# A four-layer attention kernel: Wo read in three rows a partition straight from its input, another set of streamed weight halves, local weights loaded in the second step, one local layer in the last two steps

## The chip, the cores and the metric

The kernel runs on one core of one Trainium2 chip. The metric is the device time of one execution in microseconds. A core has a matrix engine (PE, with its weight loads shown apart as PEld), DVE (VectorE), ACT (ScalarE), POOL (GpSimd), and SP (SyncE), which here only issues DMAs; sixteen DMA engines move data between the DRAM of the chip (HBM) and the on-chip memory (SBUF). PE writes its results to PSUM.

## The reference

The input x has 2048 rows of 640. Four layers follow each other, each with a layernorm ahead and the sum with its input behind:

```
def _A_ref(x, mem0, Wq, Wk, Wv, Wo, seg_len):      # H=32 heads, Dh=192, M=8, seg_len=32
    mem = mem0
    for s in range(n_seg):                          # 64 segments, one after the other
        h = concatenate([mem, xs], axis=1)          # 8 memory rows + 32 rows of x
        q, k, v = h @ Wq, h @ Wk, h @ Wv
        p = softmax(where(mask, q k^T * scale, -1e9))
        o = einsum('bhte,hed->btd', p v, Wo)
        mem = o[:, :M]; outs.append(o[:, M:])
def _B_ref(x, wqkv, wo):                            # 32 heads of 20, each row sees 8 rows,
    ...                                             # itself and every second one before it
x = x + _A_ref(_layernorm(x), ...); x = x + _B_ref(_layernorm(x), ...)
x = x + _A_ref(_layernorm(x), ...); x = x + _B_ref(_layernorm(x), ...)
```

Both A layers use the same weights, and both B layers too. A segment of an A layer needs the memory rows that the segment before it has made, so that the 64 segments are a chain.

## The kernel before

All data stand transposed, with the 640 features on 5 x 128 partitions. One step handles two segments at once: segment s of the first pair of layers (l = 0) and segment s - 2 of the second pair (l = 1, `LAG` = 2); every A matmul has 2 x 40 columns. There are 67 steps: 0 to 65 do the A layers ("attend"), 1 to 66 do the B layers for what the step before has left ("local"). Step 66 has local work alone.

The A weights are 4 x 7.5 MB and do not fit in SBUF beside the rest. They are cut into 64 halves of 128 x 1920 values (480 KB): 0 to 31 are Wk and Wq by turns, 32 to 47 Wv, 48 to 63 Wo. Of these 31 stay in SBUF from step 0 on (`res`), and 33 are streamed in every step through a ring of five buffers (`ring`, tile `wt`, `RING` = 5). Which ones are streamed is worked out by `resident_halves` (L88), which spreads them evenly over the columns that PE has to work through. In step 0, `half` (L242) loads every half from the input with `load_direct` (L238), and POOL writes each streamed one to a DRAM tile `Wr` (L253), from which the later steps read it in one run a partition (L255). A load for Wq, Wk or Wv from the input has rows of 768 bytes, one for Wo rows of 1,280 bytes.

The order of PE and SP is written out by hand: `ORDER` (L53) lists the stages of a step, and PE and SP issue in the order of that list. `q` is one pair of halves of Wk and Wq (L333, evicted by ACT at L335), `s` the scores of four of them with the softmax (L355 to L363 on DVE, exponent on ACT L359), `t` the transposition of the probabilities (PE L370, copied by DVE L372 and ACT L373 to `PT`), `v` one half of Wv (L381; the copy to `vt` is on ACT, L385, for even ones and on DVE, L387, for odd ones), `pv` probabilities times v (L398, evicted by ACT L401 to `ot`), `o` the output projection (L415), which adds up over the whole step in PSUM. `finish_step` (L418) copies the new memory rows to `ST` (L426) and makes `xr` (L439) at the end. The local stages are `ln1` (L443), `qkv` (L449; the product of q with the eight shifted k, `prod`, is on DVE for l = 0 and on POOL for l = 1, L470), `logits` (L473), `e0` to `e4` (L502: PE L505, DVE L508 and L510) and `wo` (L512). `ln2` makes the second A layer's input (L317), and `store` writes out four segments (L537). Every fourth step the next 128 rows of x are loaded to `x_sb` (L266, issued by SP at the step's beginning) and normalized in the step after (`input_tile`, L268: statistics on DVE, L274 and L275, root on ACT, L260 and L261). On DVE, ACT and POOL the order is the scheduler's: it may put an operation ahead of others that stand before it in the program.

SP issues in order: a load of a streamed half waits until PE has done with the half that was loaded five streamed halves before, and whatever stands behind it waits too. The local weights `wqkv` and `wo` are loaded at the very beginning (L571, L572), ahead of all A weights.

Of the kernel before, what the change touches and what calls it, by code (L numbers as in the profile page):

```python
# [10 lines left out]
BF16 = mybir.dt.bfloat16  # L11
# [9 lines left out]
P = 128  # L21
D = 640
# [51 lines left out]
COLUMNS = {"q": 1200, "v": 1920, "o": 1200, "s": 2000, "pv": 1000, "t": 700, "ln1": 900, "ln2": 900, "qkv": 5000, "logits": 1000, "e": 500, "wo": 1700}  # L74


def halves_of(what, i):

    if what == "q":
        return [2 * i, 2 * i + 1]  # L80
    if what == "v":
        return [32 + i]
    if what == "o":
        return [48 + i] if i < 14 else [62, 63]
    return [None]


def resident_halves():  # L88

    order, t = [], 0  # L90
    for what, i in PLAN:
        for h in halves_of(what, i):
            t += COLUMNS.get(what, 0)
            if h is not None:
                order.append((h, t))
    kept, n = set(), 0
    for h, at in order:
        if (N_HALVES - N_RESIDENT) * at >= (n + 0.5) * t:
            n += 1
        else:  # L100
            kept.add(h)
    assert len(kept) == N_RESIDENT
    return kept


RESIDENT = resident_halves()
# [9 lines left out]
def window1(ap, c):  # L116

    v = ap[:, c, :, 0:SEG]
    dims = [list(x) for x in v.ap]
    return bass.AP(v.tensor, v.offset, dims[:2] + [[BDIL, BW]] + dims[2:])  # L120
# [12 lines left out]
class Kernel:  # L133
# [94 lines left out]
    def source(self, h):  # L228
        if h < 32:
            W, i = (self.Wk, self.Wq)[h % 2], h // 2  # L230
        elif h < 48:
            W, i = self.Wv, h - 32
        else:
            i = h - 48
            return self.Wo[i * UW:(i + 1) * UW, :].rearrange("(m p) d -> p m d", p=P), 3
        return W[:, i * UW:(i + 1) * UW].rearrange("(c p) n -> p c n", p=P), NCH
# [5 lines left out]
    def half(self, h):  # L242
        if h in self.resident:
            return self.resident[h]
        if h in RESIDENT:
            t = self.res.tile([P, HALF], BF16, name=f"res{h}")
            self.load_direct(t, h)
            self.resident[h] = t
            return t
        t = self.ring.tile([P, HALF], BF16, name="wt")  # L250
        if self.step == 0:
            self.load_direct(t, h)
            self.nc.gpsimd.dma_start(out=self.Wr[h][:, :], in_=t[:, :])  # L253
        else:
            self.nc.sync.dma_start(out=t[:, :], in_=self.Wr[h][:, :])  # L255
        return t
# [118 lines left out]
    def v(self, i):  # L375
# [8 lines left out]
        if i % 2 == 0:  # L384
            nc.scalar.copy(out=vt[:, :], in_=ps[:, :])  # L385
        else:
            nc.vector.tensor_copy(out=vt[:, :], in_=ps[:, :])  # L387
        self.vts[i] = vt

    def pv(self, g):  # L390
        nc = self.nc
        for k in (2 * g, 2 * g + 1):
            ps = self.ps.tile([P, 2, 3, 2, LT], F32, name="o_ps", tag="ps")
            for jj in range(2):
                i = 2 * k + jj
                vt = self.vts.pop(i)
                for (n, slot, h, col) in ((0, 0, 0, 0), (0, 1, 0, 64), (1, 0, 0, 128), (1, 1, 1, 192), (2, 0, 1, 256), (2, 1, 1, 320)):
                    nc.tensor.matmul(ps[64 * slot:64 * (slot + 1), jj, n, :, :], lhsT=vt[:, col:col + 64], rhs=self.PT[g % 2][:, i % 4, h, :, :],  # L398
                                     start=True, stop=True, tile_position=(0, 64 * slot))
# [42 lines left out]

    def b_stats(self):  # L443
# [5 lines left out]
    def b_qkv(self):  # L449
# [18 lines left out]
        for l in range(2):  # L468
            eng = nc.vector if l == 0 else nc.gpsimd
# [3 lines left out]
    def b_logits(self):  # L473
# [3 lines left out]
        for c in range(NCH):  # L477
            for r in range(4):
                nc.tensor.matmul(ps[32 * r:32 * (r + 1), :, :], lhsT=self.E[:, c, :], rhs=self.prod[:, c, r // 2, :, hf * (r % 2):hf * (r % 2 + 1)],
# [22 lines left out]
    def b_expand(self, c):  # L502
        nc = self.nc
        ps = self.ps.tile([P, 2, BW, SEG], F32, name="bc_ps", tag="ps")
        nc.tensor.matmul(ps[:, :, :, :].rearrange("p l w t -> p (l w t)"), lhsT=self.ET[:, c, :],  # L505
                         rhs=self.attn[:, :, :, :, :].rearrange("p l w h t -> p (l w h t)"), start=True, stop=True)
        pv = self.prod[:, c, :, :, :]
        nc.vector.tensor_tensor(out=pv, in0=ps[:, :, :, :], in1=window1(self.vh, c), op=ALU.mult)  # L508
        with nc.allow_low_precision("bf16 result of an f32 sum"):
            nc.vector.tensor_reduce(out=self.oT[:, c, :].rearrange("p (l t) -> p l t", l=2), in_=pv.rearrange("p l w t -> p l t w"), op=ALU.add, axis=AX.X)  # L510

    def b_wo(self):  # L512
        nc, s = self.nc, self.step
        ps = self.ps.tile([P, NCH, 2, SEG], F32, name="y_ps", tag="ps")
        for d in range(NCH):
            for c in range(NCH):
                nc.tensor.matmul(ps[:, d, :, :].rearrange("p l t -> p (l t)"), lhsT=self.wo[:, c, d * P:(d + 1) * P], rhs=self.oT[:, c, :],  # L517
# [32 lines left out]
    def run(self):  # L550
        nc, tc = self.nc, self.tc
        self.resident, self.xt, self.vts, self.ots = {}, {}, {}, {}
        self.Wr = {h: self.dram.tile([P, HALF], BF16, name=f"Wr{h}") for h in range(N_HALVES) if h not in RESIDENT}
# [3 lines left out]
        with tc.manual_schedule(engines={PE, SP}):  # L557
# [7 lines left out]
            for s in range(n_steps + 1):  # L565
# [10 lines left out]
                for what, i in PLAN:  # L576
                    if what in attend and a:
# [66 lines left out]
```

## Time and profile before

| | us |
|---|---|
| median of 3 runs | 3621.74 (3606.78 to 3629.93) |
| the profiled execution: its own time | 3625.0 |
| its span | 3623.3 |
| PE busy, share of the span | 3410.9, 94% |
| DVE, ACT, POOL busy | 2129.0, 1506.4, 366.3 |
| DMA: bytes moved, mean rate | 1121.55 MB, 310 GB/s |
| chain that ended last: PE, DVE, DMA | 75%, 10%, 7% |

Busy time of PE is summed over the whole span, and matmuls overlap; a share of 94% does not say that PE never waits. "Issue" as a releaser means that an engine waited for nothing that the profile shows. A row of waits gives the engine and line that waited, what ended the wait, the total, how often and the longest. A row of a timeline gives the start, the duration, the engine, line, operation, tiles, shape and count, and in brackets the idle time before and what ended it.

### The profile page before, as it was taken

How to read it: one execution, taken by the hardware profiler on the slowest of the kernel's cores; microseconds unless marked ns; L12 is line 12 of the kernel's file. 1: busy time of each engine (PE TensorE's matmuls, PEld its weight loads, DVE VectorE, ACT ScalarE, POOL GpSimd, SP SyncE). 2: the span in 40 equal slices, each digit the busy share in tenths (PEclk: the TensorE clock that was granted, in tenths of full speed). 3: DMA queues.
4: the chain of work that ended last, by engine and by line, in shares of the span. 5: the costliest groups of instructions: out<-in, count | busy, mean ns of one | idle time of the engine just before them, and what ended most of it. 6: DMA issues, size and time to landing. Idle time of an engine off the chain costs nothing.

```text
span 3623.3 us, 170218 instructions
## 1 busy us (share of the span) xinstructions
PE 3410.9 (94%) x78044; PEld 2932.1 (81%) x78045; DVE 2129.0 (59%) x5056; ACT 1506.4 (42%) x3213; POOL 366.3 (10%) x467
## 2 busy tenths in 40 slices
PE   5799999999999999999999999999999999999997
PEld 3688888888888888888888887888888888888886
DVE  1356656665665665566566556556656655665565
ACT  1243444444444444444444444444444444444443
POOL 2110010111001011100101110110010111001000
PEclk6899999999999999999999999999999999999998
DMA  9998999999989998989998998899999888999995
GB/s 351 355 310 300 310 312 310 316 316 314 311 307 309 315 316 307 313 309 311 313 311 308 313 311 302 298 309 312 315 311 310 311 309 309 313 310 309 313 306 194
DMA packets 356063, 1121.55 MB, mean 310 GB/s; under 512 B 36424, under 2 KB 78032, under 8 KB 355344
## 3 DMA queue, kind: packets, MB, share of 16 engines
q1 hardware_dynamic: 350400, 1091.82, 87.7%
q8 instruction: 610, 9.99, 1.1%
q0 software_dynamic: 2640, 16.22, 1.1%
q10 hardware_dynamic: 2304, 2.62, 0.2%
q14 instruction: 109, 0.89, 0.1%
HBM read 1091.68 MB, written 18.84 MB: 306 GB/s over the span
## 4 chain that ended last, share of the span: by engine, by line
PE 75%; DVE 10%; DMA 7%; ACT 3%; issue 3%; SPq 1%; POOL 1%; POOLq 0%; DVEq 0%
PE qk_ps L333 28%; PE v_ps L381 17%; PE acc L415 11%; DMA wt<-Wr 4%; PE qkv_ps L463 4%; PE o_ps L398 2%; PE qk_ps L328 2%; PE bc_ps L505 2%; PE s_ps L351 2%; PE s_ps L345 2%; DVE vt L387 1%; PE y_ps L517 1%; PE pt_ps L370 1%; SPq L240 1%; ACT ot L401 1%
## 5 line engine op out<-in xcount | busy, mean ns | idle before, releaser
L335 ACT CAST QK<-qk_ps 128x480 bf16<-128x480 f32 x1056 | 587.3, 556 | 991.5 <-PE qk_ps L333 782.3
L333 PE MATMUL qk_ps<-ST,res 128*128 128x80 bf16 x15840 | 722.2, 203 | 23.5 <-issue 15.1
L381 PEld LDWEIGHTS <-ST 128*128 128x128 bf16 x5280 | 468.1, 99 | 275.6 <-issue 19.2
L333 PEld LDWEIGHTS <-res 128*128 128x128 bf16 x15840 | 644.4, 101 | 45.9 <-issue 18.1
L333 PE MATMUL qk_ps<-ST,wt 128*128 128x80 bf16 x13860 | 647.7, 203 | 24.6 <-DMA wt<-in_A_Wq_dram 10.6
L381 PE MATMUL v_ps<-wt,ST 128*128 128x384 bf16 x3300 | 652.6, 329 | 14.6 <-DMA wt<-in_A_Wv_dram 10.7
L333 PEld LDWEIGHTS <-wt 128*128 128x128 bf16 x13860 | 571.9, 100 | 76.6 <-DMA wt<-in_A_Wq_dram 11.6
L387 DVE CAST vt<-v_ps 128x384 bf16<-128x384 f32 x528 | 291.3, 552 | 302.9 <-PE v_ps L381 302.7
L415 PE MATMUL acc<-ot,wt 128*128 128x80 bf16 x7920 | 404.6, 203 | 46.0 <-ACT ot L401 29.7
L415 PE MATMUL acc<-ot,res 128*128 128x80 bf16 x7920 | 400.6, 203 | 15.5 <-issue 8.2
L415 PEld LDWEIGHTS <-wt 128*128 128x128 bf16 x7920 | 351.2, 100 | 69.8 <-issue 37.1
L381 PE MATMUL v_ps<-res,ST 128*128 128x384 bf16 x1980 | 392.9, 330 | 4.3 <-DMA res<-in_A_Wv_dram 3.5
L415 PEld LDWEIGHTS <-res 128*128 128x128 bf16 x7920 | 346.1, 101 | 26.4 <-issue 9.3
L401 ACT CAST ot<-o_ps 128x480 bf16<-128x480 f32 x528 | 271.0, 562 | 212.8 <-PE o_ps L398 212.7
L510 DVE TENSOR_REDUCE oT<-prod 128x64 bf16<-128x512 bf16 x330 | 339.0, 1028 | 9.0
L385 ACT CAST vt<-v_ps 128x384 bf16<-128x384 f32 x528 | 250.7, 475 | 194.9 <-PE v_ps L381 188.6
L508 DVE TENSOR_TENSOR prod<-bc_ps,vh 128x512 bf16<-128x512 f32 x330 | 226.0, 685 | 91.1 <-PE bc_ps L505 91.0
L470 POOL TENSOR_TENSOR prod<-qT,kh 128x1280 bf16<-128x1280 bf16 x66 | 204.4, 3097 | 675.4 <-ACT kh L465 675.4
L398 PE MATMUL o_ps<-PT,vt 128*64 128x80 bf16 x6336 | 163.4, 203 | 42.2 <-ACT PT L373 32.5
L298 POOL TENSOR_TENSOR sq<-x 128x160 f32<-128x160 bf16 x64 | 29.0, 452 | 1721.6 <-DVE x L521 1721.6
L361 DVE TENSOR_REDUCE sm<-sb 128x8 f32<-128x320 f32 x264 | 127.7, 484 | 110.2 <-ACT sb L359 110.2
L359 ACT ACTIVATE sb<-sb 128x320 f32<-128x320 f32 x264 | 124.1, 470 | 157.7 <-DVE sb L358 157.4
(117 smaller groups left out, 3585.7 us busy)
## 6 DMA issues: line engine op xcount, KB each, us to landing
wt<-Wr SPq DMA_DIRECT2D x2145, 480.0 KB, 5.4
Wr<-wt POOLq DMA_DIRECT2D x33, 480.0 KB, 6.5
wt<-in_A_Wv_dram SPq DMA_DIRECT2D x10, 480.0 KB, 10.3
res<-in_A_Wq_dram SPq DMA_DIRECT2D x9, 480.0 KB, 10.3
res<-in_A_Wk_dram SPq DMA_DIRECT2D x8, 480.0 KB, 10.6
wt<-in_A_Wk_dram SPq DMA_DIRECT2D x8, 480.0 KB, 9.7
wt<-in_A_Wo_dram SPq DMA_DIRECT2D x8, 480.0 KB, 10.1
res<-in_A_Wo_dram SPq DMA_DIRECT2D x8, 480.0 KB, 9.6
```

The costliest lines, as they stand in the source:

```text
L333: nc.tensor.matmul(ps[:, m, :, :], lhsT=w[m // 3][:, c, (m % 3) * P:(m % 3 + 1) * P], rhs=st[:, c, :, 0:LT], start=(c == 0), stop=(c == NC ...
L335: nc.scalar.copy(out=self.QK[i % NQK][:, 0:12 * LT], in_=ps[:, :, :, :].rearrange("p m l t -> p (m l t)"))
L381: nc.tensor.matmul(ps[:, :], lhsT=st[:, c, :, :].rearrange("p l t -> p (l t)"), rhs=w[:, c, :], start=(c == 0), stop=(c == NCH - 1))
L385: nc.scalar.copy(out=vt[:, :], in_=ps[:, :])
L387: nc.vector.tensor_copy(out=vt[:, :], in_=ps[:, :])
L398: nc.tensor.matmul(ps[64 * slot:64 * (slot + 1), jj, n, :, :], lhsT=vt[:, col:col + 64], rhs=self.PT[g % 2][:, i % 4, h, :, :], start=True ...
L401: nc.scalar.copy(out=ot[:, :, :, :], in_=ps[:, :, :, :, :].rearrange("p j n l t -> p (j n) l t"))
L415: nc.tensor.matmul(a[:, at, :, :], lhsT=w[h][:, m, dc * P:(dc + 1) * P], rhs=self.ots[h // 2][:, 3 * (h % 2) + m, :, :], start=(h == 0 and ...
L463: nc.tensor.matmul(ps[:, d, :, :], lhsT=self.wqkv[:, c, kind * D + d * P:kind * D + (d + 1) * P], rhs=self.xnB[:, c, :].rearrange("p (l t) ...
L470: eng.tensor_tensor(out=self.prod[:, :, l, :, :], in0=qT[:, :, l, :].unsqueeze(2).to_broadcast([P, NCH, BW, SEG]), in1=window(kh, l), op=A ...
L508: nc.vector.tensor_tensor(out=pv, in0=ps[:, :, :, :], in1=window1(self.vh, c), op=ALU.mult)
L510: nc.vector.tensor_reduce(out=self.oT[:, c, :].rearrange("p (l t) -> p l t", l=2), in_=pv.rearrange("p l w t -> p l t w"), op=ALU.add, axi ...
```

## The change

There are four parts.

- **Wo.** The row of Wo that partition p and block m hold is now 3p + m of a half and not 128m + p, so a partition's three rows are neighbours in DRAM: 3,840 bytes in one run, in the built program a plain 128 x 1920 copy. Streamed Wo halves are read from the input in every step, with no copy to `Wr`. The rows of `ot` have to stand in the same order, so the copies of `v_ps` to `vt` read PSUM at every third element and write three blocks of 128, and in `pv` the half of the probabilities is that of the output slot.
- **Streamed halves.** The set is a list: 11 of Wk and Wq, 9 of Wv, 13 of Wo, where before it was 15, 10 and 8. The number, 33, and the ring stay.
- **Local weights.** `wqkv` is loaded in three parts at the beginning of step 1, `wo` ahead of stage q8 of step 1.
- **Steps 65 and 66.** Only l = 1 has local work there. The logits for l = 0 are made from l = 1's product, `prod`, `e0` to `e4` and `wo` do half as much, and in step 66 the product of l = 1 is on DVE.

```
-RESIDENT = resident_halves()
+STREAMED = (
+    1, 2, 6, 9, 11, 12, 14, 17, 20, 25, 31, 32, 33, 34, 35, 36, 39, 40, 43, 44, 48, 49, 50, 51, 52, 53, 54, 55,
+    56, 57, 58, 59, 60,
+)
+RESIDENT = set(range(N_HALVES)) - set(STREAMED)
...
-            return self.Wo[i * UW:(i + 1) * UW, :].rearrange("(m p) d -> p m d", p=P), 3
+            return self.Wo[i * UW:(i + 1) * UW, :].rearrange("(p m) d -> p m d", p=P), 3
...
         t = self.ring.tile([P, HALF], BF16, name="wt")
-        if self.step == 0:
+        if h >= 48:
+            self.load_direct(t, h)
+        elif self.step == 0:
             self.load_direct(t, h)
             self.nc.gpsimd.dma_start(out=self.Wr[h][:, :], in_=t[:, :])
...
-            nc.scalar.copy(out=vt[:, :], in_=ps[:, :])
+            nc.scalar.copy(out=vt[:, :].rearrange("t (m p) -> t m p", m=3), in_=ps[:, :].rearrange("t (p m) -> t m p", m=3))
         else:
-            nc.vector.tensor_copy(out=vt[:, :], in_=ps[:, :])
+            nc.vector.tensor_copy(out=vt[:, :].rearrange("t (m p) -> t m p", m=3), in_=ps[:, :].rearrange("t (p m) -> t m p", m=3))
...
-                for (n, slot, h, col) in ((0, 0, 0, 0), (0, 1, 0, 64), (1, 0, 0, 128), (1, 1, 1, 192), (2, 0, 1, 256), (2, 1, 1, 320)):
-                    nc.tensor.matmul(ps[64 * slot:64 * (slot + 1), jj, n, :, :], lhsT=vt[:, col:col + 64], rhs=self.PT[g % 2][:, i % 4, h, :, :],
+                for n, slot in ((n, slot) for n in range(3) for slot in range(2)):
+                    col = P * n + 64 * slot
+                    nc.tensor.matmul(ps[64 * slot:64 * (slot + 1), jj, n, :, :], lhsT=vt[:, col:col + 64], rhs=self.PT[g % 2][:, i % 4, slot, :, :],
...
+    def layers(self):
+
+        return (0, 1) if self.step <= self.n_seg else (1,)
...
-        for l in range(2):
-            eng = nc.vector if l == 0 else nc.gpsimd
+        for l in self.layers():
+            eng = nc.vector if l == 0 or self.step > self.n_seg + LAG - 1 else nc.gpsimd
...
     def b_expand(self, c):
         nc = self.nc
+        ls = slice(self.layers()[0], 2)
...
-        nc.vector.tensor_tensor(out=pv, in0=ps[:, :, :, :], in1=window1(self.vh, c), op=ALU.mult)
+        nc.vector.tensor_tensor(out=pv, in0=ps[:, ls, :, :], in1=window1(self.vh, c, ls), op=ALU.mult)
...
-                if s == 0:
-                    nc.sync.dma_start(out=self.wqkv[:], in_=self.B_wqkv.rearrange("(c p) n -> p c n", p=P))
-                    nc.sync.dma_start(out=self.wo[:], in_=self.B_wo.rearrange("(c p) n -> p c n", p=P))
+                if s == 1:
+                    for kind in range(3):
+                        ks = slice(kind * D, (kind + 1) * D)
+                        nc.sync.dma_start(out=self.wqkv[:, :, ks], in_=self.B_wqkv[:, ks].rearrange("(c p) n -> p c n", p=P))
...
                 for what, i in PLAN:
+                    if s == 1 and (what, i) == ("q", 8):
+                        nc.sync.dma_start(out=self.wo[:], in_=self.B_wo.rearrange("(c p) n -> p c n", p=P))
```

More of the change, by code (lines that the diff above doesn't have):

```diff
@@ L71 @@
 PLAN = stages()
[L74 to L103, printed above, removed]
-RESIDENT = resident_halves()
+STREAMED = (
[3 more added lines that the diff above has]
+RESIDENT = set(range(N_HALVES)) - set(STREAMED)
+assert len(RESIDENT) == N_RESIDENT
 def window(ap, l):
@@ L113, in window, with window1 @@
     return bass.AP(v.tensor, v.offset, dims[:2] + [[BDIL, BW]] + dims[2:])
-def window1(ap, c):
-    v = ap[:, c, :, 0:SEG]
+def window1(ap, c, ls):
+    v = ap[:, c, ls, 0:SEG]
     dims = [list(x) for x in v.ap]
@@ L478, in b_logits @@
             for r in range(4):
-                nc.tensor.matmul(ps[32 * r:32 * (r + 1), :, :], lhsT=self.E[:, c, :], rhs=self.prod[:, c, r // 2, :, hf * (r % 2):hf * (r % 2 + 1)],
+                nc.tensor.matmul(ps[32 * r:32 * (r + 1), :, :], lhsT=self.E[:, c, :], rhs=self.prod[:, c, max(r // 2, self.layers()[0]), :, hf * (r % 2):hf * (r % 2 + 1)],
                                  start=(c == 0), stop=(c == NCH - 1), tile_position=(0, 32 * r))
@@ L516, in b_wo @@
             for c in range(NCH):
-                nc.tensor.matmul(ps[:, d, :, :].rearrange("p l t -> p (l t)"), lhsT=self.wo[:, c, d * P:(d + 1) * P], rhs=self.oT[:, c, :],
+                nc.tensor.matmul(ps[:, d, ls, :].rearrange("p l t -> p (l t)"), lhsT=self.wo[:, c, d * P:(d + 1) * P], rhs=self.oT[:, c, SEG * ls.start:],
                                  start=(c == 0), stop=(c == NCH - 1))
@@ L552, in run @@
         self.resident, self.xt, self.vts, self.ots = {}, {}, {}, {}
-        self.Wr = {h: self.dram.tile([P, HALF], BF16, name=f"Wr{h}") for h in range(N_HALVES) if h not in RESIDENT}
+        self.Wr = {h: self.dram.tile([P, HALF], BF16, name=f"Wr{h}") for h in range(48) if h not in RESIDENT}
         self.kh = self.vh = None
```

9 lines of the change are left out of this document (5 added, 4 removed).

## The prediction

> **What bounds the kernel now.** I cut the span at the first matmul of L328, with which each step begins: 66 starts, the first at 16.4 us, the second at 144.7, then every 52.9 us on the mean, the last at 3540.6; step 66 (local layer alone) runs from 3593.3 to 3623.3. The table by stretches gives, for step 0, step 1, a middle step, step 65 and step 66, the length, each engine's busy time, the granted clock, the DMA share and GB/s:
>
> ```profile
> 16.40:144.70 128.30, 78.57 (x1040) 58.02 (x1040) 16.89 (x39) 20.21 (x40) 19.05 (x38) 0.68 1.07 367
> 144.70:198.10 53.40, 52.03 (x1183) 45.17 (x1182) 33.03 (x82) 22.69 (x50) 5.01 (x6) 0.97 0.93 324
> 1733.30:1785.90 52.60, 50.57 (x1182) 43.76 (x1179) 31.57 (x76) 22.50 (x48) 5.08 (x6) 1.00 0.91 312
> 3540.60:3593.30 52.70, 50.05 (x1173) 43.17 (x1169) 29.99 (x68) 22.25 (x46) 4.31 (x4) 1.00 0.84 282
> 3593.30:3623.30 30.00, 11.16 (x145) 7.88 (x142) 14.21 (x32) 2.89 (x7) 3.75 (x2) 0.60 0.02 7
> ```
>
> Three regimes: step 0 is DMA (share 1.07: two queues overlap on the engines; PE busy 78.57 of 128.30), steps 1 to 65 are PE, step 66 is a chain of small operations. For the steady steps I next read PE's waits between 250 and 3540 us (62 steps; total, times, longest):
>
> ```profile
> PE o_ps L398 <- ACT PT L373: 31.1, 57, 0.7
> PE acc L415 <- ACT ot L401: 28.9, 62, 0.7
> PE qk_ps L333 <- issue: 21.0, 28, 2.4
> PE acc L415 <- issue: 12.8, 17, 1.8
> PE o_ps L398 <- issue: 9.5, 12, 1.9
> PE v_ps L381 <- DMA wt<-Wr: 2.6, 8, 0.5
> ```
>
> The first two are the softmax chain that ends each step, about 1 us a step. Weights that arrive late cost only 6.3 us in all (2.6 here, 2.0 at L415, 1.7 at L333). "issue" is 48.4 us with its smaller rows. It stands in the middle of runs of matmuls, where no semaphore is waited for:
>
> ```profile
> 1753.46 0.60 PE L415 MATMUL acc<-ot,wt 128*128 128x80 bf16 x12
> 1755.05 0.27 PE L415 MATMUL acc<-ot,wt 128*128 128x80 bf16 x3 [0.98 <-issue]
> ...
> q8 instruction: 610, 9.99, 1.1%
> ```
>
> The instruction queue moved 9.99 MB in 610 packets of 16,384 bytes; PE and PEld have 156,089 instructions, 256 to a packet. I read this idle time as PE out of instructions while their transfer stands behind weights. Of its 47.8 us in steps 10 to 59, 29.4 lie 16 to 24 us into the step (stages q8 to o1).
>
> **The change part by part.** PE's count of matmuls is the same, so the steady 50.75 us of a step without any idle time (sum of the shortest times of its stages) stays.
>
> *Step 0.* Its terms are DMA time, from packet durations in the trace over 16 engines. Wo: 384 packets of 1,280 B at 59 ns are 1.42 us a half; the new load is one run of 3,840 B a partition, 128 at 149 ns, 1.19 us: 16 x 0.23 = 3.6 us. Copies to DRAM: the software queue holds 27.1% of the first 144.7 us, 39.2 us for 33 copies, 1.19 each; 13 fewer are 15.5 us. The local weights leave: 640 x 165 ns / 16 + 640 x 58 ns / 16 = 6.6 + 2.3 = 8.9 us. Sum 28.0; the 151 us of packet time of this stage passed in 144, a factor of 0.95: 26.7. I take 25, since the first copy can't start before POOL has made its constants (first one issued at 16.3 us, landed 23.1), while the weights now arrive 9 us earlier and the ring of five is full before. The lower bound is 10: SP waited 28.1 us here for slots that a copy held (18.7 + 9.4 in SP's waits), and if that wait grows with the denser streaming up to v4 (13 halves of 23, 12 before), most of the rest is lost.
>
> *Step 1.* The three loads of wqkv stand on SP's queue ahead of the step's x_sb and first weights, and behind the last loads of step 0, in a queue that is full: 3 x 640 x 59 ns / 16 = 7.1 us by which q0 of step 1 comes later. Nothing covers it; PE is done with step 0 some 2 us after its last weight. Bounds 0 and 9.5 (with wo). wo (2.3 us) goes in ahead of q8, in a steady step whose waits for weights are small: 1, bounds 0 and 2.3. So steps 0 and 1 give 25 - 7.1 - 1 = **17 us**.
>
> *Steps 65 and 66.* The last stretch shows the local chain of step 66:
>
> ```profile
> 3602.07 0.83 DVE L470 TENSOR_TENSOR prod<-qT,kh 128x1280 bf16<-128x1280 bf16 x1 [3.37 <-ACT kh L465]
> 3602.18 3.03 POOL L470 TENSOR_TENSOR prod<-qT,kh 128x1280 bf16<-128x1280 bf16 x1 [7.20 <-ACT kh L465]
> ...
> 3605.26 0.46 PE L479 MATMUL lg_ps<-prod,E 128*32 128x128 bf16 x18 [2.08 <-POOL prod L470]
> ```
>
> With layer 1's product on DVE the logits start at 3602.95 instead of 3605.26: 2.3 us. L508 and L510 go from 512 elements to 256: L508 from 0.68 to 0.42 (L521 takes 0.33 for 160: 1.02 ns an element), L510 from 1.03 to 0.58 (half of all above 0.14, which is what L300's 0.72 and 0.43 for 320 and 160 leave). 5 x 0.71 = 3.5 us, all on the chain. The first bc_ps, half as long, 0.2. In step 65 five bc_ps lose half of 0.22 us: 0.5. Sum **6.5 us**, bounds 4 and 8.
>
> *The order on DVE.* The scheduler hoists the layernorm statistics of the next input tile (L274) to the end of every fourth step. Before, they stand behind the last vt and PT copies; in the changed program, in 14 such steps, ahead of both, behind L317. The rows of one such step before:
>
> ```profile
> 776.35 0.33 DVE L317 TENSOR_TENSOR ST<-xc,ln_r 128x160 bf16<-128x160 f32 x1 [0.65 <-ACT ln_r L261]
> 776.59 0.55 DVE L387 CAST vt<-v_ps 128x384 bf16<-128x384 f32 x1
> 777.06 0.30 DVE L372 COPY PT<-pt_ps 64x320 bf16<-64x320 bf16 x1
> 778.36 0.89 DVE L274 BATCH_NORM_STATS2 bst<-x_sb 128x6 f32<-128x320 bf16 x2 [1.00 <-DMA x_sb<-in_A_x_dram]
> ```
>
> L274 waits for x_sb. Put at 776.7 it would block DVE until 778.36 and 0.89 longer. Behind it are vt15 and PT, then ACT's PT half, pv3 and the last projection: PE waits for all of it. Over the 14 steps x_sb landed 2.0 us after L317's end on the mean, so the cost would be 2.9 us. But x_sb leaves SP earlier: the last streamed half now takes the slot of v12, not of o8, which PE frees 0.7 us sooner, and one transfer fewer lies ahead of it (1.2 us between landings). I take 1.4 us (0.5 + 0.9), bounds 0.9 and 2.9. Those steps gain back 0.25 us each, by which they were longer than the others (53.24 to 53.0). 14 x 1.4 - 3.5 = **16 us lost**, bounds 9 and 37.
>
> *The set of streamed halves.* Still 33 a step, ring of five. The uses v4 q9 q9 o0, four streamed ones in a run, become v4 and then o0 o1 behind two resident ones; qkv is followed by q6 v2 with a resident half between. At the end of the step o8 to o12 come in a row. I take a third of the 29.4 us from the "issue" idle time, scaled to 64 steps less what the later runs cost: **8 us gained**, bounds 35 gained (most of it and the late weights) and 12 lost.
>
> *vt and pv.* The copies of v_ps read PSUM at every third element. For DVE a strided PSUM read is in the trace: L490 reads lg_ps at a stride of 16 elements in 281 ns and the same shape from SBUF in 370 ns, and 281 is 128 elements at the 1.04 ns of L387 (552 ns for 384, 0.15 fixed). So 0, with an upper bound of double the 0.40 us that scale. ACT has no such row; its vt14 ends 0.7 us before its PT half, which hides up to that. The matmuls of pv now always take different rows of PT in a pair; before, one pair in three did, and its starts are 34 ns apart against 32: 0. [...]
>
> **Sum.** -17 - 6.5 + 16 - 8 = -15.5 us (0.4%). The profiled execution took 3625.0 us, span 3623.3; the sum gives 3609.5 for it. The median of the runs is 3.3 lower: **3606 us**. About 1%, 36 us, is what a measurement can tell from no change.
>
> **The rivals.** (a) *The even stream pays in full*: PE's "issue" and weight waits fall by 35, and x_sb lands before L274 needs it (9 lost): -17 - 6.5 + 9 - 35 = -49.5, 3572. For it: 29.4 us at one place. Against: late weights cost little. (b) *x_sb comes no earlier*: 37 lost instead of 16: 3627; for it, x_sb took 5.7 us to land. (c) *The ring holds step 0*, so that it gives 10 instead of 25: 3621; against, the DMA share is over 1 there. (d) *Strided copies of v_ps are slow on DVE*, which ends slower than before: vt13 and vt15 stand in the chain to PT one behind the other (L387, L309, L317, L387), so 0.40 us each are 0.8 us x 65 steps = 52: 3658. It turns the sign from 0.12 us a copy on. [...]
>
> **Chances.** Forecast 0.52, (a) 0.20, (b) 0.12, (c) 0.06, (d) 0.10. The range takes in (b) and (c), most of (a)'s side, and half the way to (d): 3576 to 3642. Faster by over 1% (under 3585.5): (a) and a little of the forecast, 0.23; slower by over 1%: (d) at its full size, 0.08; within 1%: 0.69.
>
> **What the profile of the changed kernel would show.** Step 1 begins near 120 us and its first matmuls wait some 7 us for DMA. In 14 steps DVE waits at the statistics' line for x_sb in front of vt, and PE's longest waits for ACT's PT half grow from 0.7 to about 2 us. "issue" rows of PE shrink a little. Step 66 takes 24 us. vt copies keep 550 and 479 ns. I am wrong if the steady steps change by more than 0.3 us each, if step 0 ends after 130 us, or if vt is slower.

## The result, and the profile after

The changed kernel takes 3660.18 us (median of 4 runs, 3657.87 to 3661.62) where the kernel before takes 3617.77 beside it (4 runs, 3606.78 to 3629.93). The ratio is 1.0103, 95% interval 1.0075 to 1.013: slower by 1%, where the forecast was 0.4% faster, and 18 us above the range. The profiled execution took 3660.96 us with a span of 3659.3, so 36.0 us of span have to be found against the 3623.3 of before.

The table by stretches of the kernel after, cut again at the first matmul of a step, which is now at L304. It shows step 0, step 1, two steady steps in a row (the first of them prepares a next input tile), step 65 and step 66. The columns are those of the table shown of before: length, busy time of PE, PEld, DVE, ACT and POOL, granted clock, DMA share, GB/s.

```profile
16.40:120.50 104.10, 68.40 (x1041) 50.73 (x1041) 16.51 (x38) 20.28 (x40) 12.01 (x25) 0.80 1.07 367
120.50:184.00 63.50, 52.35 (x1183) 45.15 (x1180) 33.66 (x82) 22.98 (x50) 5.01 (x6) 0.95 0.94 326
940.70:997.90 57.20, 52.36 (x1181) 45.29 (x1178) 33.25 (x82) 22.97 (x50) 5.07 (x6) 0.97 0.89 301
997.90:1051.10 53.20, 50.66 (x1186) 43.87 (x1184) 31.78 (x76) 22.38 (x48) 5.08 (x6) 1.00 0.87 295
3585.40:3636.10 50.70, 49.95 (x1177) 43.40 (x1173) 26.19 (x68) 22.01 (x46) 3.67 (x4) 1.00 0.84 290
3636.10:3659.30 23.20, 8.92 (x143) 7.00 (x139) 10.62 (x32) 2.88 (x7) 0.72 (x1) 0.65 0.02 8
```

Step 0 is 24 us shorter, step 1 is 10 us longer, and step 66 is 7 us shorter. The steady step 940.7 to 997.9 takes 57.2 us. Step 16 of before, the same one, took 53.1. The step that follows it is an ordinary one. Summed over the traces, with steps 2 to 64 sorted by their number modulo four (16, 15, 16 and 16 steps):

| us | before | after | difference | forecast |
|---|---|---|---|---|
| step 0 | 128.3 | 104.0 | -24.2 | -25 |
| step 1 | 53.4 | 63.6 | +10.2 | +8.1 |
| steps 4, 8, ... 64 (14 of the 16 prepare an input) | 53.24 each | 55.92 each | +42.9 | +16 |
| the other 47 steady steps | 52.99 each | 53.33 each | +16.0 | -8 |
| steps 65 and 66 | 82.7 | 73.9 | -8.8 | -6.5 |
| span | 3623.3 | 3659.3 | +36.0 | -15.5 |

So the loss is in the steady steps, and most of it in every fourth one. PE's waits of the kernel after between 250 and 3540 us (total, times, longest):

```profile
PE o_ps L375 <- ACT PT L349: 67.2, 60, 3.7
PE acc L392 <- ACT ot L378: 28.2, 61, 0.6
PE acc L392 <- issue: 22.8, 17, 2.4
PE qk_ps L309 <- issue: 20.8, 27, 1.8
...
PE acc L392 <- DMA wt<-in_A_Wo_dram: 3.5, 9, 0.6
```

The wait of pv for ACT's half of PT has gone from 31.1 to 67.2 us, and its longest from 0.7 to 3.7. "issue" in all its rows has gone from 48.9 to 57.4. The other waits stand as before. The timeline of the end of step 16 shows the wait (start, duration, engine, line, operation; in brackets the idle time before and what ended it):

```profile
989.78 0.32 DVE L293 TENSOR_TENSOR ST<-xc,ln_r 128x160 bf16<-128x160 f32 x1 [0.65 <-ACT ln_r L237]
...
991.01 0.89 DVE L250 BATCH_NORM_STATS2 bst<-x_sb 128x6 f32<-128x320 bf16 x2 [0.91 <-DMA x_sb<-in_A_x_dram]
991.82 0.54 DVE L363 CAST vt<-v_ps 128x384 bf16<-128x384 f32 x1
992.27 0.31 DVE L348 COPY PT<-pt_ps 64x320 bf16<-64x320 bf16 x1
...
993.09 0.62 PE L375 MATMUL o_ps<-PT,vt 128*64 128x80 bf16 x24 [2.50 <-ACT PT L349]
...
995.17 2.95 PE L392 MATMUL acc<-ot,res 128*128 128x80 bf16 x45
```

The queue on DVE is the one that the prediction describes: after L293 comes an idle 0.91 us for x_sb, then the statistics, then vt and PT. PE stands still for 2.50 us. What the prediction does not have is the last row: 45 matmuls take 2.95 us, where before 15 of them follow the next 15 by 0.53 us, 1.6 for 45. The granted clock (third column from the end) in stretches of 2 us of the same place says why:

```profile
990.00:992.00 2.00, 0.59 (x17) 0.56 (x14) 1.09 (x4) 0.11 (x1) 0.00 (x0) 1.00 0.92 350
992.00:994.00 2.00, 0.62 (x24) 0.59 (x24) 1.04 (x5) 1.30 (x4) 0.00 (x0) 1.00 0.97 349
994.00:996.00 2.00, 1.78 (x28) 1.77 (x28) 0.27 (x1) 0.63 (x2) 0.00 (x0) 0.57 0.49 193
996.00:998.00 2.00, 2.00 (x38) 2.00 (x36) 0.40 (x3) 0.00 (x0) 0.00 (x0) 0.58 0.78 230
998.00:1000.00 2.00, 2.00 (x62) 2.00 (x59) 1.09 (x5) 0.56 (x1) 0.72 (x1) 1.00 0.04 15
```

PE is busy for 1.2 us of the four from 990 to 994. Right behind them the clock is granted at half for some 3.4 us, and then it is back at 1.00. Cut into stretches of 2 us, the time between 220 and 3520 us shows 14 such places ("halved windows" below) in the kernel after and 3 in the kernel before. Twelve of the 14 stand behind the wait for PT.

The length of the wait alone does not decide this. In the clock records of this trace each of the 14 halved windows is 3,413 ns long and all of them start on one grid of 3,413 ns. Between 220 and 3520 us there are 967 windows of that grid; the 13 in which PE was busy for less than 0.45 of the time were all followed by half clock, and of the other 954 one was (busy 0.59). So a wait of 3.01 us that fell across two windows (busy 0.47 and 0.50, step 32) was not followed by half clock, and one of 2.11 us was (0.37, step 48). In the kernel before, the windows ahead of the three halved ones have PE busy for 0.38, 0.46 and 0.54.

Two rows of step 66 of the kernel after answer to the forecast of the last steps, and two views by source line to that of the copies of v_ps (minimum, median and maximum in ns, over all 528 of a line):

```profile
3652.75 0.41 DVE L490 TENSOR_TENSOR prod<-bc_ps,vh 128x256 bf16<-128x256 f32 x1
...
3653.20 0.58 DVE L492 TENSOR_REDUCE oT<-prod 128x32 bf16<-128x256 bf16 x1
```

```profile
L363 DVE CAST vt<-v_ps x528: 540/551/559, 33.7 to 3631.6; 128x384 bf16<-128x384 f32 x176
...
L361 ACT CAST vt<-v_ps x528: 458/478/512, 26.0 to 3630.9; 128x384 bf16<-128x384 f32 x176
```

Before, the two copies took 550 and 479 ns. Reading PSUM at every third element cost neither engine anything here, so the rival that ended on the slower side is not what made this kernel slower.

### The profile page after: what moved, and what is told of

It is laid out like the page before. It is cut to its first block, busy times and chain, and to the rows that moved or that the text cites. A ratio compares the mean times of both kernels' runs of the same rounds, so it can differ in the third digit from the quotient of the medians.

```text
span 3659.3 us, 170138 instructions
## 1 busy us (share of the span) xinstructions
PE 3414.5 (93%) x78045; PEld 2938.3 (80%) x78045; DVE 2122.2 (58%) x5055; ACT 1502.5 (41%) x3213; POOL 354.9 (10%) x453
## 3 DMA queue, kind: packets, MB, share of 16 engines
q8 instruction: 609, 9.98, 1.1%
## 4 chain that ended last, share of the span: by engine, by line
PE 72%; DMA 11%; DVE 9%; ACT 3%; issue 3%; POOL 1%; SPq 0%; POOLq 0%; DVEq 0%; ACTq 0%
PE qk_ps L309 27%; PE v_ps L357 17%; PE acc L392 12%; DMA wt<-Wr 4%; PE qkv_ps L444 4%; DMA wt<-in_A_Wo_dram 2%; PE qk_ps L304 2%; DMA x_sb<-in_A_x_dram 2%; PE o_ps L375 2%; PE bc_ps L487 2%; PE s_ps L327 2%; PE s_ps L321 2%; DVE vt L363 1%; PE y_ps L500 1%; PE pt_ps L346 1%
## 5 line engine op out<-in xcount | busy, mean ns | idle before, releaser
L309 PE MATMUL qk_ps<-ST,res 128*128 128x80 bf16 x19800 | 871.3, 202 | 27.7 <-issue 19.7
L309 PEld LDWEIGHTS <-res 128*128 128x128 bf16 x19800 | 796.7, 100 | 84.3 <-issue 25.0
L392 PE MATMUL acc<-ot,wt 128*128 128x80 bf16 x12870 | 584.0, 203 | 64.3 <-ACT ot L378 30.3
L357 PE MATMUL v_ps<-wt,ST 128*128 128x384 bf16 x2970 | 589.5, 330 | 13.6 <-DMA wt<-in_A_Wv_dram 6.4
L309 PE MATMUL qk_ps<-ST,wt 128*128 128x80 bf16 x9900 | 467.9, 203 | 14.6 <-DMA wt<-in_A_Wq_dram 9.5
L357 PE MATMUL v_ps<-res,ST 128*128 128x384 bf16 x2310 | 445.3, 328 | 5.7 <-DMA res<-in_A_Wv_dram 3.5
L492 DVE TENSOR_REDUCE oT<-prod 128x64 bf16<-128x512 bf16 (+1 forms) x330 | 334.6, 1014 | 9.0
L490 DVE TENSOR_TENSOR prod<-bc_ps,vh 128x512 bf16<-128x512 f32 (+1 forms) x330 | 223.7, 678 | 96.8 <-PE bc_ps L487 96.2
L375 PEld LDWEIGHTS <-vt 128*64 128x64 bf16 x6336 | 143.1, 114 | 76.8 <-issue 71.8
L349 ACT COPY PT<-pt_ps 64x320 bf16<-64x320 bf16 x264 | 110.9, 420 | 172.9 <-DVE PT L348 166.5
```

Source lines behind the costliest of these rows:

```text
L309: nc.tensor.matmul(ps[:, m, :, :], lhsT=w[m // 3][:, c, (m % 3) * P:(m % 3 + 1) * P], rhs=st[:, c, :, 0:LT], start=(c == 0), stop=(c == NC ...
L357: nc.tensor.matmul(ps[:, :], lhsT=st[:, c, :, :].rearrange("p l t -> p (l t)"), rhs=w[:, c, :], start=(c == 0), stop=(c == NCH - 1))
L392: nc.tensor.matmul(a[:, at, :, :], lhsT=w[h][:, m, dc * P:(dc + 1) * P], rhs=self.ots[h // 2][:, 3 * (h % 2) + m, :, :], start=(h == 0 and ...
L490: nc.vector.tensor_tensor(out=pv, in0=ps[:, ls, :, :], in1=window1(self.vh, c, ls), op=ALU.mult)
```

## The experiments

The theory after the two traces: what is lost comes of the order on DVE in 14 steps, partly as a wait and partly as the halved clock behind it, and the order comes of the new set of halves. Rivals: the set costs by itself (late weights, or instructions that come late), reading Wo from the input costs in each step, and what step 0 gains is paid elsewhere. Ten kernels ran, in three groups. Each ratio is to the kernel before on the same chip beside it. That one took 3624.23 us in the group of the order put back, the earlier load, the new set alone and the earlier set; 3629.12 in that of PE kept busy, no loads, the local weights and the second layernorm; 3628.3 in that of the two spread sets.

### The order on DVE put back

```
-        for s_ in range(2):
-            nc.vector.bn_stats(...)
+        if t > 0:
+            with self.tc.issue_after(self.pt3):   # the last PT copy of the step on DVE
+                for s_ in range(2):
+                    nc.vector.bn_stats(...)
...
-        self.rsqrt(st[:, 1:2], st[:, 2:3])
+        if t > 0:
+            with self.tc.issue_after(self.ot3):   # the last ot copy of the step on ACT
+                self.rsqrt(st[:, 1:2], st[:, 2:3])
...
```

> The changed kernel, with the statistics of the next input tile (L274 of before) tied behind the last PT copy on DVE and their root behind the last ot copy on ACT, as the kernel before had them; the load of x_sb and all else stay. Theory A (the moved statistics cost some 42 us: PE sits idle 2.4 us in 14 steps and then has a stretch at half clock): 3618 us, within 8; the steps with s%4==0 fall from 55.9 to about 53.3 us, no half-clock window in steady steps. Theory B (the set of streamed halves and the direct reads of Wo cost the time, and the statistics only move a wait): 3655 to 3662, the steps with s%4==0 stay above 55.

Measured: 3625.02 us, ratio 1.0005 (0.9987 to 1.0023). Theory A holds. The timeline at the end of one of the 14 steps, with the statistics behind the last vt and PT copies again:

```profile
983.22 0.55 DVE L374 CAST vt<-v_ps 128x384 bf16<-128x384 f32 x1
...
983.92 0.87 DVE L252 BATCH_NORM_STATS2 bst<-x_sb 128x6 f32<-128x320 bf16 x2
...
984.50 0.62 PE L386 MATMUL o_ps<-PT,vt 128*64 128x80 bf16 x24 [0.72 <-ACT PT L360]
```

PE's idle time is 0.72 us in place of 2.50, the clock is halved in one window in place of 14, and the steps that prepare an input take 53.46 us. Against the kernel after this is 0.0098 of the time, 35 us, for the order alone (with the two intervals, 24 to 47). But it also leaves a puzzle: with step 0 and the last steps won and the order back, the kernel is only as fast as before, not faster.

### The input asked for sooner, the order left

```
-                if s % 4 == 1 and 4 * (s // 4 + 1) < self.n_seg:
-                    self.input_load(s // 4 + 1)
...
+                    if s % 4 == 0 and (what, i) == ("v", 4) and 4 * (s // 4 + 1) < self.n_seg:
+                        self.input_load(s // 4 + 1)
```

The statistics are tied behind the operation that precedes them in the kernel after, and so keep their place ahead of vt and PT; only x_sb is there in time.

> The changed kernel's order on DVE and ACT, but SP issues x_sb ahead of v4 of the step before, so that it has landed when the statistics come. Theory A: DVE is held for the 0.9 us of the two statistics alone, 14 x 0.9 = 13 us over the order of before; PE idles some 1.6 us there and the clock stays full: 3618 + 13 = 3631 us (3625 to 3637). If 1.6 us of idle time already halve the clock: 3640 to 3650. Theory B: 3655 to 3662.

Measured: 3639.93 us, ratio 1.0045 (1.0028 to 1.0062): of the 35 us that the order costs, 21 (1.0103 to 1.0045) go when x_sb is there in time, and 14 stay. This is above the 3625 to 3637 us that was expected for a clock that stays full, and at the lower end of the 3640 to 3650 for one that halves. The execution that was profiled was the fastest of ten, 3626.28 us, and near the first experiment's: in it the wait for PT is 48.9 us in all, the longest 1.5, and the clock is halved in 3 windows. So x_sb's lateness is the larger part by the runs and nearly all by the trace. PE's idle time ahead of pv is 1.5 us in each of the 14 steps, and two of them (steps 4 and 44) are followed by half clock: there PE was busy for 0.45 of the grid's window, where the lowest share without half clock behind it is 0.48. Whether the other nine executions lost the 14 us to the statistics themselves (0.9 us in 14 steps are 12.5) or to more halved windows cannot be read from one trace.

### PE kept busy through the wait

The order of the kernel after, and 50 matmuls of 128x80 into a PSUM tile that nothing reads ahead of the last pv in the 14 steps:

```
+        if g == 3 and self.step % 4 == 0 and 0 < self.step < 60:
+            self.fill(50)
         for k in (2 * g, 2 * g + 1):
```

> The changed kernel with 50 extra matmuls (128x80, into a PSUM tile that nothing reads) on TensorE just ahead of the last group of pv in the 14 steps that prepare a next input; the last groups' statistics stay ahead of PT on VectorE, so PT is as late as before. 45 such matmuls took 1.6 us at full clock, so the extra work is about 1.8 us and lies inside the 2.4 us in which TensorE stood idle there. Theory A (the drop of the granted clock to 0.5 follows the long idle of TensorE and costs time beside the wait): the half-clock windows fall from 14 to 5 or fewer, and the time falls by 14 x about 1 us, to 3640 to 3650. Theory B (the half-clock windows come of something else, or cost nothing beside the wait): 3657 to 3665, with 12 or more windows.

Measured: 3648.87 us, ratio 1.0059 (1.0042 to 1.0075), with 3 halved windows, one of them in the 14 steps (step 52). The extra matmuls and the clock in stretches of 2 us, at the end of the same step:

```profile
985.55 1.96 PE L370 MATMUL fill_ps<-ST,ones_b 128*128 128x80 bf16 x50
986.30 0.89 DVE L250 BATCH_NORM_STATS2 bst<-x_sb 128x6 f32<-128x320 bf16 x2 [1.08 <-DMA x_sb<-in_A_x_dram]
...
988.38 0.62 PE L383 MATMUL o_ps<-PT,vt 128*64 128x80 bf16 x24 [0.87 <-ACT PT L349]
```

```profile
987.00:989.00 2.00, 1.13 (x39) 1.05 (x36) 1.07 (x5) 1.02 (x4) 0.32 (x1) 1.00 0.95 323
989.00:991.00 2.00, 1.49 (x42) 1.50 (x43) 0.52 (x2) 0.92 (x2) 0.00 (x0) 1.00 0.52 205
```

PT is as late as in the kernel after (DVE waits 1.08 us for x_sb), but the clock stays at 1.00, and the kernel is faster for doing more work. Theory A holds: the halved clock cost 11.6 us by the spans (3659.3 to 3647.7), 16 by the ratios. In the traces the sixteen steps in which the 14 lie are 14.9 us shorter (879.8 for 894.7); step 1, with the same instructions, happened to take 2.6 us more. With the order put back the same steps take 855.4, so that the wait itself is the larger price: 24 of the 39 us.

In the kernel after, the idle times ahead of pv in the 14 steps were 2.11 to 3.71 us, and 12 of the 14 were followed by half clock. With the input asked for sooner, two of 14 idle times of 1.5 us were followed by it too.

### The new set alone

The kernel before with the list of streamed halves and nothing else of the change; Wo is copied and read as before.

```
-RESIDENT = resident_halves()
+STREAMED = (1, 2, 6, 9, 11, 12, 14, 17, ...)      # the list of the change
+RESIDENT = set(range(N_HALVES)) - set(STREAMED)
```

> The kernel before with nothing but the new set of streamed halves (Wo still copied to DRAM, local weights in step 0, both layers to the end). The scheduler moves the statistics ahead of vt and PT here as in the changed kernel. Theory A: 3618 + 42 for the order + 16 for what the other steady steps lost = 3676 us (3665 to 3685). Theory B, where the set itself costs all 59 us of the steady steps: the same total, but the excess spread over all steps and not in s%4==0. If the direct reads of Wo are what costs: 3618 to 3635.

Measured: 3681.77 us, ratio 1.0154 (1.0121 to 1.0186), as expected. Its steady steps 2 to 64 take 3395.4 us (3401.4 in the kernel after, 3342.5 before), and PE's wait for PT is the same as after:

```profile
PE o_ps L372 <- ACT PT L347: 63.7, 60, 3.9
```

So the set alone moves the statistics on DVE and makes the loss, with 16 halved windows. It lies where theory A puts it: the sixteen steps of which 14 prepare an input take 48.1 us more than before, the other 47 steps 4.9. The 6.0 us that the kernel after takes beyond this are within what two traces can differ by (see the local weights below), so reading Wo from the input rather than from its copy costs the steady steps nothing that can be told here.

### The earlier set in the changed kernel

```
-STREAMED = (...)
-RESIDENT = set(range(N_HALVES)) - set(STREAMED)
+RESIDENT = resident_halves()
```

Eight halves of Wo are then streamed, read from the input; the order on DVE is that of before without any tie.

> The changed kernel with the set of streamed halves of before (8 of Wo, read directly); the statistics stand behind vt and PT again by themselves. Theory A: -14 (steps 0 and 1) and -9 (last steps) against before, steady steps as before: 3595 us (3585 to 3605). If direct reads of Wo or the strided vt copies cost the steady steps: 3605 to 3620, all steps longer than 52.9. Step 0 has 25 copies to DRAM and not 20, 6 us more than in the changed kernel, which may take 3600.

Measured: 3612.57 us, ratio 0.9967 (0.9951 to 0.9983): faster than both kernels, by less than expected (3585 to 3605). The time lies in the range given for direct reads or strided copies that cost the steady steps, but these are no longer than before: 52.96 us each on the mean, 53.06 before. The profiled execution, 3605.22, is one of the faster ones. Against the first experiment (the new set with the order put back) step 0 is 6.5 us longer, for five copies more; its steady steps are 24.0 us shorter (3336.4 against 3360.4). So the set costs even without the order on DVE: by the ratios 13.8 us of the whole, and 20 with the difference of step 0 added. PE's waits of the first experiment, the new set:

```profile
PE qk_ps L318 <- issue: 20.1, 26, 2.8
PE acc L405 <- issue: 16.0, 15, 1.8
PE v_ps L368 <- issue: 9.4, 8, 2.5
PE v_ps L368 <- DMA wt<-Wr: 8.1, 16, 1.7
...
PE acc L405 <- DMA wt<-in_A_Wo_dram: 5.3, 13, 1.0
```

and of this one, the earlier set:

```profile
PE qk_ps L335 <- issue: 15.8, 21, 2.0
PE acc L418 <- issue: 14.1, 16, 2.2
...
PE acc L418 <- DMA wt<-in_A_Wo_dram: 4.0, 9, 0.9
...
PE v_ps L383 <- DMA wt<-Wr: 1.7, 2, 1.5
```

In all rows "issue" is 56.0 us with the new set and 42.9 with the earlier one, and waits for weights are 15.6 and 7.9: together 20.8 of the 24.0.

### No weight loads at all

What is behind "issue"? The first experiment's kernel, with no streamed half loaded from step two on:

```
     def half(self, h):
+        if self.step >= 2:
+            self.nth += 1
+            return self.last5[self.nth % RING]
```

> The changed kernel with the order on VectorE and ScalarE of before, and no streamed weight half loaded from step two on: the last five tiles of the ring are used again, so that the output is that of other weights; what is left out is 33 loads a step and every wait for them. Theory A (the idle of TensorE that the profile puts down to issue is its instruction fetch kept waiting behind the weight loads): issue falls from 56 us to under 10 us, the DMA waits from 15.6 us to 0, and the time to 3540 to 3560. Theory B (issue is inherent in the instruction stream and only the late weights go): issue stays at 45 to 60 us and the time is 3605 to 3612.

Measured: 3516.17 us, ratio 0.9693 (0.9667 to 0.9718), 24 us below what even theory A expected. PE's waits; the rows below these two are of 3.0 us and less, each ended by DVE:

```profile
PE o_ps L390 <- ACT PT L364: 41.0, 62, 1.0
PE acc L409 <- ACT ot L393: 29.1, 63, 0.6
```

Two executions ran. There is no row of "issue" left (56.0 us in the first experiment), although the instruction queue moves as much as before (9.98 MB in 609 packets, for 156,090 instructions of PE and PEld: 256 a packet). So this idle time is not a property of the instruction stream. The records of the packets in the trace say when each starts. I set this against the time at which PE reaches a fixed instruction (the 190th of each block of 256), and against the stall that PE shows 260 instructions further on, where the stalls sit. Without loads the packet starts 0.1 us later on the mean. In the kernel after it starts 0.9 us later while less than half a weight half is outstanding on the queue (counted from the least seen), 1.8 with 1 to 1.5 halves, 2.8 with 2 to 2.5, and 3.3 with more; the stall grows from 0 to 0.27 us a block. Where these waits stand points the same way: counted in blocks of 256, all 71 waits of PE for "issue" before and all 64 after stand ahead of the 194th or 195th instruction of a block. Summed from 200 us to 3540 these stalls are 58 us before, 66 after, 68 in the first experiment, and 2 here. So the instruction packets wait behind the weights here: 0.9 to 3.3 us by the backlog, for 0.1 without loads. In the steady steps the weight stream costs 3360.4 - 3257.3 = 103 us, 3%. "Issue" and late weights are 72 of it (56.0 and 15.6); where the rest comes from is open.

### The local weights back in step zero

The kernel with the earlier set, and

```
-                if s == 1:
-                    for kind in range(3): ...
+                if s == 0:
+                    nc.sync.dma_start(out=self.wqkv[:], ...)
+                    nc.sync.dma_start(out=self.wo[:], ...)
...
-                    if s == 1 and (what, i) == ("q", 8): ...
```

> The changed kernel with the earlier set of streamed halves, and with the local weights loaded in step zero as before, so that against the kernel with the earlier set alone only the place of those loads differs. Theory A (what step zero gains by the move, step one pays back for lack of a cover): step zero 118 to 121 us in place of 110.3, step one 53 to 55 in place of 64.9, the whole 3610 to 3615. Theory B (the move is worth its share of step zero): 3618 to 3625.

Measured: 3603.45 us, ratio 0.9939 (0.9919 to 0.9959). In the stretches, steps 0 and 1 of this kernel:

```profile
16.40:136.80 120.40, 75.33 (x1040) 56.37 (x1040) 17.27 (x40) 20.07 (x40) 14.72 (x30) 0.72 1.06 366
136.80:188.80 52.00, 50.85 (x1183) 44.18 (x1181) 32.80 (x79) 22.43 (x50) 5.01 (x6) 0.99 0.91 312
```

and of the kernel with the earlier set, loads in step one:

```profile
16.40:126.70 110.30, 72.74 (x1038) 54.73 (x1038) 16.31 (x38) 20.09 (x40) 14.83 (x31) 0.71 1.06 367
126.70:191.60 64.90, 54.34 (x1184) 46.70 (x1181) 33.73 (x83) 23.02 (x50) 5.02 (x6) 0.89 0.90 314
```

Step 0 loses 10.1 us and step 1 gains 12.9. By the stages theory A holds, and by the time the kernel is even a little faster than it expects (the profiled execution, 3614.44, took 11 us more than the median). The move gains nothing: step 1 pays the loads once as a wait of 7.7 us at its first matmul, and again at a granted clock of 0.89 in place of 0.99:

```profile
PE qk_ps L330 <- DMA wt<-Wr: 7.7, 1, 7.7
```

These two traces also show how much a single trace can tell. From step 2 on the two kernels are the same, and their steady steps take 3350.0 and 3336.4 us: 13.6 us of difference between two executions.

### The second layernorm later

The kernel with the earlier set, and one line of the written order:

```
-s3 pv2 v12 o8 v13 ln20 o9 v14 v15 t3 o10 o11 store0 pv3 o12 o13 o14
+s3 pv2 v12 o8 v13 o9 v14 v15 t3 o10 o11 ln20 store0 pv3 o12 o13 o14
```

> The changed kernel with the earlier set of streamed halves, and ln20 put behind t3, o10 and o11 in the written order, so that the last copy of PT in a step is no longer queued on VectorE behind the second layer norm. Theory A (the 38 us that pv waits for PT in the steady steps come of that queue): the wait falls to under 15 us and the time to 3575 to 3595. Theory B (the second layer norm is needed just as early by what follows: the end of a step waits for it instead): the wait for PT falls but as much comes up at the first matmuls of the next step or at o, 3608 to 3618.

Measured: 3603.56 us, ratio 0.9923 (0.9901 to 0.9945). The three waits at the turn of a step were 37.9, 28.6 and 2.4 us (PT, ot, ST) with the earlier set; the first is gone, and the other two are

```profile
PE acc L418 <- ACT ot L404: 39.9, 61, 1.4
...
PE qk_ps L330 <- DVE ST L429: 20.5, 14, 2.0
```

That is 60.4 us for 68.9: theory B in the trace, where the steady steps are the same (3336.8 and 3336.4). The ratio is 0.0044 lower than that of the earlier set, across two groups of runs, and lies between the theories; the size of the gain is not settled.

### Thirteen halves of Wo, spread

```
 RESIDENT = resident_halves()
+SWAPS = ((20, 49), (38, 50), (26, 52), (42, 54), (46, 57))
+RESIDENT = (RESIDENT | {a for a, b in SWAPS}) - {b for a, b in SWAPS}
```

> The changed kernel with 13 streamed halves of Wo as in the change, but spread: the earlier set with five of its halves (20, 38, 26, 42, 46) given up for the Wo halves used nearest to them (49, 50, 52, 54, 57). The statistics on VectorE stand behind vt and PT as in the kernel with the earlier set. Theory A (the steady steps lose by the spacing of the change's set, pairs and runs of streamed uses): issue stays near 43 to 48 us and late weights near 8 to 10, steady steps 2 to 64 at 3335 to 3345 us, step zero near 104 as with the other set of 13, the whole 0.993 to 0.997 of the kernel before. Theory B (13 Wo halves streamed cost by their number, whatever the spacing): issue 52 to 58 us, steady 3355 to 3365, the whole at 0.999 to 1.002.

Measured: 3619.39 us, ratio 0.9975 (0.9962 to 0.9989). Steady steps 3355.5 us, and "issue" 53.8 and late weights 13.5 us in all, are theory B's; the ratio lies between the two theories. By the traces the spread set is worse than the earlier one by 19.1 us of steady steps. By the ratios (0.0008, 2.9 us, with 5.3 us less in step 0 and 2.9 less in step 1) it is worse by about 11. The change's own set is worse by 24.0 and, worked out in the same way, by 20. So more than the spacing is at work; that spacing is a part of it is likely and not shown, since 5 us of traces and 9 of ratios are hardly beyond the noise. How the rest comes of having more halves of Wo among the 33 is open.

### The spread set with the second layernorm later

The two edits above together.

> The same set with ln20 behind t3, o10 and o11 in the written order. Theory A (the two gains add up): 3 to 8 us under the kernel with the spread set alone, 0.990 to 0.995 of the kernel before. Theory B (the wait for PT turns into waits for ot and ST of the same size): the same as the spread set alone within 3 us.

Measured: 3627.06 us, ratio 0.9996 (0.9981 to 1.001): not faster than the spread set alone but 0.2% slower. Theory B, and 4.7 us worse than its 3 us allow. Two rows show what took the place of the wait for PT:

```profile
PE acc L421 <- ACT ot L407: 39.9, 61, 1.4
...
PE acc L421 <- DMA wt<-in_A_Wo_dram: 19.8, 39, 2.1
```

In the spread set alone these were 28.9 and 7.8. No gain of this edit carries from one set to the other.

## Why the prediction was wrong, step by step

- **Step 0: right.** -24.2 for -25. The prices hold in the experiments: with the earlier set there are five copies more and step 0 takes 6.3 us more than in the kernel after (1.26 each for 1.19), and the local weights are 10.1 us for 8.9. SP's wait for slots held by a copy went from 28.1 to 22.1 us, so the ring did not hold it.
- **Step 1: right in kind, 2 us too small.** +10.2 for +8.1. The wait is 7.0 us as worked out (7.1). The granted clock of the step fell from 0.97 to 0.95, which is 1.6 us more over its length, and no term stood for that:

```profile
PE qk_ps L304 <- DMA wt<-Wr: 7.0, 1, 7.0
```

- **Steps 65 and 66: right.** -8.8 for -6.5. Step 66 gives 6.8 (30.0 to 23.2), with L490 at 0.41 and L492 at 0.58 us where 0.42 and 0.58 were worked out. Step 65 gives 2.0 where 0.5 was seen.
- **The order on DVE: wrong in size, +42.9 for +16.** The mechanism and the 14 steps were right. Two things were missing. First, the wait for x_sb behind L293 was taken as 0.5 us; it is 1.11 on the mean (0.53 to 2.12; 2.07 before), and PE's idle time ahead of pv rose from 0.59 to 2.70 us a step: 2.1 in place of 1.4, 30 us. Second, in 12 of the 14 steps PE was now busy for only 0.16 to 0.40 of a 3.4 us window, and the window behind it was granted half clock: 12 to 16 us by the experiment with PE kept busy. The 0.25 us a step that these steps were to gain back is not seen.
- **The set of streamed halves: wrong in sign.** -8 was predicted. The steady steps that prepare no input lost 16.0 us (4.9 with the set alone), and with the order put back the new set costs 24.0 us of steady steps against the earlier one by the traces, about 20 by the ratios. These sizes are rough, since two traces of the same steps differed by 13.6; the sign is not. PE's waits for "issue" and for weights together are 50.8 to 57.0 us in the four traces with the earlier set and 59.7 to 71.6 in the five with the new one and its loads. The prediction read rightly that "issue" is PE out of instructions behind the weights; the experiment without loads shows it (56.0 us with the loads, no such row without). It went wrong in the next step: it took one run of uses that disappeared (v4 q9 q9 o0) as a third of the idle time saved, and gave the new pairs a small price. (Its 29.4 of 47.8 us are 26.0 of 39.0 when waits of over 0.15 us in steps 10 to 59 are added up; the place is right.) The stall moved within the step. By the time into a step at which a block is due, stalls at 12 to 16 and 16 to 20 us were 28.0 and 8.8 us before, and are 14.4 and 19.9 after: one place halved, the next doubled, together 36.8 and 34.3; and all others went from 21.5 to 32.2.
- **vt and pv: right.** 551 and 478 ns, for 550 and 479 before. The doubling in the bound of that term and in the rival of slow copies is shown by no run.
- **The sum.** Against the forecast, steps 0, 1, 65 and 66 together are 0.6 us worse (-22.8 for -23.4), and the two wrong terms make up the rest of the 51.5 us: 26.9 for the order on DVE and 24.0 for the set. Of the rivals, "x_sb comes no earlier" is nearest, at 37 us for the order; but x_sb did come earlier by about a microsecond, and the clock made up for it. No rival had the steady steps losing by the set; the bounds of that term went to 12 us lost. The rival of slow copies had 3658, nearly the time measured, and that was chance: its cause is not there.

## What to carry to other kernels

Before changing which transfers a kernel streams, look at what a scheduler does to the order on the engines in consequence: here a changed list of halves moved a 0.9 us instruction that waits for a DMA ahead of the copies on which the matrix engine depends, and that was worth 35 us of 3,620, more than all that the change was made of. A wait of the matrix engine had two prices here: its own length, and half clock for 3.4 us behind it. In the kernel after, half clock followed each of the 13 windows of that length in which PE was busy for less than 0.45; with the input asked for sooner, two waits of 1.5 us were enough. When loads are moved out of a stage that is bound by DMA, look for what covers them in the stage that takes them: step 1 had no cover, and paid back all of it (12.9 us, for 10.1 won in step 0 with the earlier set).

## What the runs showed of the hardware that was not expected

- The granted clock fell to half for one window of about 3.4 us behind idle times of PE of 2.1 to 3.7 us in 12 of 14 cases, and behind ones of 1.5 us in 2 of 14. What went with it was PE's busy share in the 3,413 ns window just before: all 13 windows under 0.45 in the kernel after, and one of 954 above (0.59); in the kernel before the three were at 0.38, 0.46 and 0.54. Fifty matmuls in each of 14 steps, which compute nothing that is used, made the kernel 12 us faster by the span.
- The 156,090 instructions of PE and PEld came in 609 DMA packets, 256 each, and these waited behind the weights. In the kernel after, at a mean of 305 GB/s, a packet starts 0.9 to 3.3 us after PE has reached the 190th instruction of a block, by the backlog, and 0.1 us after it without loads. PE was idle for "issue" for 43 to 57 us of 3,290 in the kernels with the loads, and not at all in the one without.
- Copies from PSUM at every third element (12 bytes apart) take 551 ns on DVE and 478 on ACT, where copies of one run took 550 and 479.
- The earlier set, with Wo read directly and the last step for one layer, is faster than both kernels: 0.9967 (0.9951 to 0.9983), with the local weights back in step 0 it is at 0.9939 (0.9919 to 0.9959), and with the second layernorm later at 0.9923 (0.9901 to 0.9945).
